# Block-sparse attention and a gated FFN on one core: half of the batches by lists of key blocks instead of dense masked scores

## The chip, the core and the metric

One core of a Trainium2 chip runs the whole program. The metric is device time in microseconds (us); the median of three runs of the kernel before is 308.7 us. Engines in the profile: PE multiplies matrices (PEld loads its weights), DVE and ACT do elementwise work, ACT also exponentials, POOL is the general engine that also issues some transfers, SP only issues transfers. All five work through their own fixed list of instructions in order and wait for each other by semaphores.

## The reference

```python
# q, k, v: (4 batches, 8 heads, 768 positions, 64); blocks of 32 positions, 24 blocks
scores = q @ k.T / 8
mask   = |block_i - block_j| <= 1, or block_i or block_j is 0 or 23,
         or block_j is one of three sampled blocks of block_i (the same for all batches and heads)
attn   = softmax(where(mask, scores, -1e9));  x = attn @ v          # heads side by side: (3072, 512)
xn     = x / rms(x) * rms_g
out    = (silu(xn @ w_gate) * (xn @ w_val)) @ w_out                 # 512 -> 1536 -> 512
```

A row of a block between 1 and 22 attends to at most 8 of the 24 blocks (itself and two neighbours, the first, the last, three sampled); rows of blocks 0 and 23 attend to all.

## The kernel before

The work is cut into *units* of query positions: batch 0 into three units of 128 rows and one of 384, batches 1 to 3 into two of 384 each, ten units in all (0 to 9). Attention runs by pairs of heads.

Attention is dense, and the mask costs no extra instruction: q and k get 24 further columns (kmask and the row of the block matrix, DVE fills `aug`), so that the score product adds -32768 where the mask forbids. For a pair, `load` fetches k, q, v; `fill` casts k and q into `aug`; `turn` transposes `aug` into a slot `X` by a DMA transpose (batch 0 by PE, `tpx`, `evx`); `pad_v` casts v into `vaug`, whose 65th column is 1, so that the weighted sum also gives the softmax's denominator.

- `qk` (L276): scores, 128 keys by up to 384 queries in one matmul; `exp` (L296): ACT takes the exponential of 768 columns of PSUM.
- `av` (L310): 65 columns wide, the exponentials are the weights; `xo` (L321, L322): DVE divides by the denominator.
- `sq` (L335), `rsq` (L343, POOL), `xq` (L350): RMS norm. `tr` (L361) and `cp` transpose the unit by PE for units 0 to 3, `xt` by a DMA transpose for later ones (`NPET = 4`).
- FFN: `proj` (L388) for g and v, `th` (L397, ACT), `uu` (L403) and `hp` (L414, DVE), `yy` (L427) the second product, `yo` (L437) the scaling, then the store.

PSUM has eight banks: scores use two pairs of banks, g bank 4, v bank 5, y bank 6, the weighted sums bank 7. So g and v of one step wait until DVE has read the step before.

No engine order is written by hand. `op(key, engines with costs, dependencies, priority, function, acquires, releases)` describes each step, and a planner in Python picks, step by step, the one that can start first by its own costs and due times; the result is one fixed list for each engine. Batch 0 attention comes first, with little FFN beside it; from unit 3 on, the attention of later units is woven into the FFN of earlier ones; after about 222 us only FFN is left. Loads run on SP in a fixed sequence `seq`, a new one starting when its buffer is free (`raw` has three).

The lines that copy (L108 ACT, L110 POOL, L112 DVE) are those of the helper `copy`.

Of the kernel before, what the change touches and what calls it, by code (L numbers as in the profile page):

```python
# [17 lines left out]
def kernel(  # L18
# [11 lines left out]
):  # L30
    nc = tc.nc
    SIMOUT = None
# [12 lines left out]
    NSLOT, NAUG, NRAW, NOPEN = 5, 2, 3, 2  # L45
# [6 lines left out]
    UNITS += [(b, c, 3) for b in range(1, B) for c in (0, 3)]  # L52
    NU = len(UNITS)
    HG = [(b, c // 3) for b, c, n in UNITS]
# [3 lines left out]
    raw = ctx.enter_context(tc.tile_pool(name="raw", bufs=NRAW))  # L58
    work = ctx.enter_context(tc.tile_pool(name="work", bufs=2))
    psum = ctx.enter_context(tc.tile_pool(name="psum", bufs=1, space=bass.MemoryType.PSUM))  # L60
    PS = psum.tile([P, 8, 512], FP32, name="PS")

# [7 lines left out]
    raws = {}  # L70
    aug = [const.tile([P, 2, 2, NC, P], BF16, name=f"aug{i}") for i in range(NAUG)]
    XA = const.tile([P, NSLOT, 2, 2, S], BF16, name="XA")
    X = [XA[:, i] for i in range(NSLOT)]
    vaug = [const.tile([P, H * NC, D + 2], BF16, name=f"vaug{i}") for i in range(2)]

    def load(g, i):
        b, pr = divmod(g, NP)
        if i == 0:
            raws[g] = raw.tile([P, 3, 2, NC * D], FP32, name="qkv", tag="qkv")
        nc.sync.dma_start(out=raws[g][:, i], in_=(kv, qv, vv)[i][b, :, 2 * pr:2 * pr + 2, :])  # L80
# [9 lines left out]
    A = [raw.tile([P, 3, 2, NC * D], FP32, name="qkv", tag="qkv") for g in range(3)]  # L90
# [23 lines left out]
    zt = const.tile([P, 512], BF16, name="zt")  # L114
# [11 lines left out]
    def idle(n, bk=7):  # L126
# [23 lines left out]
        base=-(NB - 1), pattern=[[0, 32]], channel_multiplier=1)  # L150
    kt_ = bank16(4)[:, 0:S].rearrange("p (c t) -> p c t", t=P)
# [8 lines left out]
    for t in vaug:  # L160
        nc.vector.memset(t[:, :, D:D + 1], 1.0)
# [71 lines left out]

    def fill(g, i, eng):
        copy(eng, aug[g % NAUG][:, i, :, :, 0:D],
             raws[g][:, i].rearrange("p h (c d) -> p h c d", d=D))

    def pad_v(g, eng):
        b, pr = divmod(g, NP)
        src = raws.pop(g) if b else A[g]  # L240
        copy(eng, vaug[b % 2][:, 2 * pr * NC:2 * (pr + 1) * NC, 0:D],
             src[:, 2].rearrange("p h (c d) -> p (h c) d", d=D))
# [21 lines left out]

    pts, xos, xns, hps, mss, xqs, tiles = {}, {}, {}, {}, {}, {}, {}
    KT, FG = {1: 3, 2: 2, 3: 1}, {1: 3, 2: 2, 3: 1}

    def qk(u, pr, g, bk):
        b, c0, nt = UNITS[u]
        x, kt, w = X[(b * NP + pr) % NSLOT], KT[nt], nt * P  # L270
        s_ = PS[:, bk[0]:bk[0] + 2]
        tiles["s", u, pr, g] = s_
        for e in range(2):
            for j in range(kt):
                jt = g * kt + j
                nc.tensor.matmul(  # L276
                    out=s_[:, e, j * w:(j + 1) * w],
                    lhsT=x[0:KQ, 0, e, jt * P:(jt + 1) * P],
                    rhs=x[0:KQ, 1, e, c0 * P:c0 * P + w], start=True, stop=True)

    def exp(u, pr, g):
        b, c0, nt = UNITS[u]
        kt, w = KT[nt], nt * P
        if (u, pr) not in pts:
            if nt == 1:
# [4 lines left out]
                else:  # L290
                    t_ = work.tile([P, 2, NC, 2, w], BF16, name="pt", tag="pt", bufs=NPT)
                pts[u, pr // 2 * 2], pts[u, pr // 2 * 2 + 1] = t_[:, 0], t_[:, 1]
            else:
                pts[u, pr] = work.tile([P, NC, 2, w], BF16, name="pt", tag="pt", bufs=NPT)
# [6 lines left out]
    def av(u, pr, bk):  # L301
        b, c0, nt = UNITS[u]
        pt, va = pts.pop((u, pr)), vaug[b % 2]
# [11 lines left out]
    def xo(u, pr):  # L315
        nt = UNITS[u][2]
        if u not in xos:
            xos[u] = work.tile([P, nt, H, D], FP32, name="xo", tag="xo")
# [4 lines left out]
            out=xos[u][:, :, 2 * pr:2 * pr + 2, :], in0=o_[:, :, :, 0:D],  # L323
            in1=rz.unsqueeze(3).to_broadcast([P, nt, 2, D]), op=ALU.mult)

    def sq(u, t):
        nt = UNITS[u][2]
# [3 lines left out]
        i, z = 0 if nt == 1 else t, slice(0, DM)  # L331
        if nt == 1:
            z = (slice(0, 3 * DM // 4), slice(3 * DM // 4, DM))[t]
        x = xos[u][:, i].rearrange("p h d -> p (h d)")[:, z]
        nc.vector.tensor_tensor_reduce(  # L335
            out=sc[:, z], in0=x, in1=x, scale=1.0 / DM, scalar=mss[u][:, 0:1] if nt == 1 and t else 1e-6,
            op0=ALU.mult, op1=ALU.add, accum_out=mss[u][:, t:t + 1])

    def rsq(u):
        nt = UNITS[u][2]  # L340
        r = work.tile([P, nt], FP32, name="rs", tag="rs")
        x = mss[u][:, 1:2] if nt == 1 else mss[u]
        nc.gpsimd.tensor_tensor(out=r, in0=x, in1=nhalf[:, 0:nt], op=ALU.pow)  # L343
        mss[u] = r

    def xq(u, t):
        nt = UNITS[u][2]
        if u not in xqs:
            xqs[u] = work.tile([P, nt, DM], BF16, name="xq", tag="xq")
        nc.vector.scalar_tensor_tensor(  # L350
            out=xqs[u][:, t, :], in0=xos[u][:, t].rearrange("p h d -> p (h d)"),
# [12 lines left out]
    def cp(u, eng):  # L364
        nt = UNITS[u][2]
        xns[u] = work.tile([P, nt, NP, P], BF16, name="xn", tag="xn", bufs=NXN)
        o, i = xns[u], tiles.pop(("tr", u))[:, 0:nt]
        if eng == "ACT":
            nc.scalar.copy(out=o, in_=i)
        else:  # L370
            nc.vector.tensor_copy(out=o, in_=i)

    def xt(u):
# [4 lines left out]
            in_=xqs[u].rearrange("p t f -> p (t f)"))  # L378

# [27 lines left out]
    def hp(u, f):  # L407
        nt = UNITS[u][2]
        fg = FG[nt]
        if u not in hps:  # L410
            if HG[u] not in hps:
                hps[HG[u]] = work.tile([P, NF, 3 * P], BF16, name="hp", tag="hp", bufs=NHP)
            hps[u] = hps[HG[u]][:, :, UNITS[u][1] % 3 * P:(UNITS[u][1] % 3 + nt) * P]
# [17 lines left out]
    def yo(u, t, h, eng):  # L431
        b, c0, nt = UNITS[u]
        y_ = tiles.pop(("yp", u, t, h))
        n = y_.shape[1]
        o = work.tile([P, n], FP32, name="yo", tag="yo", bufs=3)
# [4 lines left out]
        dst = out[b * S:(b + 1) * S, :].rearrange("(p c) f -> p c f", c=NC)  # L440
        nc.sync.dma_start(out=dst[:, c0 + t, h * n:(h + 1) * n], in_=o)

    NPT, NXN, NHP, NPET = 3, 3, 2, 4
    pools = {n: [0.0] * c for n, c in (
        ("pt", NPT), ("hp", NHP), ("xo", 2), ("xq", 2), ("xn", NXN), ("raw", NRAW), ("va0", 1),
        ("va1", 1), ("th", 2), ("uu", 3))}
    for i in range(NSLOT):
        pools[f"X{i}"] = [0.0]
    for i in range(NAUG):
        pools[f"aug{i}"] = [0.0]  # L450
# [3 lines left out]
    held = {}  # L454
    LAT = {"PE": 0.2, "ACT": 0.16, "DVE": 0.08, "POOL": 0.1, "DMA": 1.9, "DMA2": 2.0}
    ops, end, made = [], {}, {}

    def op(key, engs, deps, prio, fn, acq=(), rel=(), at=0.0):
        o = dict(key=key, engs=engs, deps=deps, prio=prio, fn=fn, acq=acq, rel=rel, at=at,
                 n=len(ops))  # L460
# [5 lines left out]
    def ld0(key, d, fn=None, deps=(), acq=(), rel=()):  # L466
        op(key, {"DMA": d}, list(deps), (0,), fn, acq, rel)
        seq.append(key)

    for g in range(NP - 1):  # L470
        held["raw", g] = "raw"
        pools["raw"].pop()
# [17 lines left out]

    prev = None
    for i in range(NWC + NOC):
# [15 lines left out]
        seq.append(("w", i))  # L508
        if i >= NWC - 1:
            seq += [("ld", NP + i - NWC + 1, j) for j in range(3)]  # L510
    seq += [("ld", g, i) for g in range(2 * NP - 1, B * NP) for i in range(3)]
    in_seq = set(seq)
# [5 lines left out]
    for g in range(NP):  # L518
        a_ = g % NAUG
        rr = [("raw", g)] if g < NP - 1 else []  # L520
# [3 lines left out]
        for n_, (es, lo, hi) in enumerate(QP[g == 0]):  # L524
            dep = ("q2",) if lo == 3 else ("l", 0, 1, n_) if g == 0 else ("l", g, 1)
            pri = (-1, g, 1) if lo == 0 else (2.5, g, lo)
# [4 lines left out]
        for i in range(2):  # L531
            for n_, (es, lo, hi) in enumerate((KP, QP)[i][g == 0]):
# [3 lines left out]
                else:  # L536
                    pri = (-1, g, 1) if lo == 0 else (2.5, g, lo)
# [16 lines left out]
    for r_ in "KQR":  # L554
        for a_ in range(2):
            pools[f"a{r_}{a_}"] = [0.0]
    held["aK0", 0] = "aK0"
# [3 lines left out]
    for g in range(NP, B * NP):  # L561
        b, pr = divmod(g, NP)
        gate = {NP: 2, NP + 1: 3, NP + 2: 4, NP + 3: 5}.get(g)
        for i in range(3):
            def ld(e, p, g=g, i=i, gate=gate):
# [3 lines left out]
            op(("ld", g, i), {"DMA": 1.1}, [("w", gate)] if gate is not None and i == 0 else [],  # L569
               (1,), ld, [("raw", g)] if i == 0 else [])  # L570
# [4 lines left out]
            else:  # L575
                op(("pv", g), {"DVE": 0.57}, [("ld", g, 2), ("fill", g, 0), ("fill", g, 1)],
                   (4, g, 2), lambda e, p, g=g: pad_v(g, e), [(f"va{b % 2}", b)], [("raw", g)])
        op(("turn", g), {"DMA": 4.6}, [("fill", g, 0), ("fill", g, 1)], (-1, g),
           lambda e, p, g=g: turn(g), [(f"X{g % NSLOT}", g)], [(f"aug{g % NAUG}", (g, False))])

# [9 lines left out]

    for u, (b, c0, nt) in enumerate(UNITS):
        w, last = nt * P, c0 + nt == NC
        ng = NC // KT[nt]
        for pr in range(NP):
            g0 = b * NP + pr
            pk = pr // 2 if nt == 1 else pr
            ptn = ("hp", "ph") if u == 0 and pk == 1 else ("pt", (u, pk))
            for g in range(ng):
                op(("qk", u, pr, g), {"PE": 2 * KT[nt] * mm(w)}, dep0(g0, b, c0, nt, KT[nt], g),
                   (2 if u else 0.5, u, pr, g), lambda e, p, a=(u, pr, g): qk(*a, p),  # L600
                   [(S3 if u < NOPEN else S_, ("s", u, pr, g)), ptn],
                   [(f"X{g0 % NSLOT}", g0)] if last and g == ng - 1 else [])
                op(("exp", u, pr, g), {"ACT": 0.075 + 2 * KT[nt] * w / 1200.0},
                   [("qk", u, pr, g)], (3, u, pr, g), lambda e, p, a=(u, pr, g): exp(*a),
                   [], [(None, ("s", u, pr, g))])
            op(("av", u, pr), {"PE": nt * 12 * 0.0325},
               [("exp", u, pr, g) for g in range(ng)] + [("pv", g0)]
               + ([("av", u, pr - 1)] if nt == 1 and pr % 2 else []), (1, u, pr),
               lambda e, p, a=(u, pr): av(*a, p), [([(7,)] + [(6,)] * (u < 3), ("o", u, pr)), ("xo", u)],
               ([ptn] if nt > 1 or pr % 2 else []) + ([(f"va{b % 2}", b)] if last and pr == NP - 1 else []))  # L610
            op(("xo", u, pr), {"DVE": 0.4 + w / 960.0}, [("av", u, pr)], (0, u, pr),
               lambda e, p, a=(u, pr): xo(*a), [], [(None, ("o", u, pr))])
        ns = max(nt, 2)
        for t in range(ns):
# [185 lines left out]
```

## Time and profile before

| | us |
|---|---|
| runs | 308.39, 308.70, 309.43 (median 308.7) |
| span of the profiled execution (first to last instruction) | 307.2 |
| median less span: what lies around it | 1.5 |
| PE, ACT, DVE, POOL busy | 299.6, 203.7, 192.3, 24.4 |
| ACT in the dense exponentials (192 of 128x768, about 812 ns each) | 145.8 |

The profiled execution has a span of its own and no separate time; changes are worked out in it and carried to the median. Busy PE time counts modelled ends of pipelined matmuls; the chain of work that ended last, in order of time, gives the spacing of matmuls. A line of a group reads: line, engine, operation, out<-in, shapes, count, then busy us, mean ns of one, idle time before them and what ended it. A line of a stretch reads: from:to, length, then busy time (and instructions) of PE, PEld, DVE, ACT, POOL, granted clock, share of the DMA engines, GB/s.

### The profile page before, as it was taken

What the parts mean: (1) busy time and instruction counts of PE and PEld (TensorE: products, weight loads), DVE (VectorE), ACT (ScalarE), POOL (GpSimd) and SP (SyncE); (2) the same over time, 40 slices, a digit from 0 to 9 for tenths busy, and PEclk for the clock granted to TensorE, in tenths of its full rate; (3) what the DMA queues carried; (4) which work ended last, traced back from release to release, by engine and by line L of the source; (5) the groups of instructions that cost most, each with busy time, mean ns of one, the idle gap of its engine ahead of it and who ended that gap; (6) DMA issues with size and microseconds to landing.
All of it is one profiled execution on the core that took longest, in us unless ns stands there. A gap on an engine that the chain in (4) does not pass through costs nothing.

```text
span 307.2 us, 7350 instructions
## 1 busy us (share of the span) xinstructions
PE 299.6 (98%) x3033; PEld 200.2 (65%) x3062; DVE 192.3 (63%) x435; ACT 203.7 (66%) x319; POOL 24.4 (8%) x43
## 2 busy tenths in 40 slices
PE   8999999999999999999999999999999999999994
PEld 7998888766666566666666666666666546556543
DVE  6687766857779678756754753674389607727500
ACT  5999875678977878787877787878833143233221
POOL 3566000100001001001000100010000000000000
PEclk9999999999999999999999999999999999999999
DMA  7999999999999999940894030003010050010022
GB/s 207 370 231 172 215 268 228 228 333 247 262 285 271 227 205 222 242 155 3 173 157 101 0 87 2 34 3 85 2 36 1 20 158 12 0 70 0 0 105 104
DMA packets 70661, 42.42 MB, mean 138 GB/s; under 512 B 48356, under 2 KB 67556, under 8 KB 70628
## 3 DMA queue, kind: packets, MB, share of 16 engines
q1 hardware_dynamic: 64528, 37.17, 49.2%
q0 software_dynamic: 5792, 4.72, 10.0%
q8 instruction: 24, 0.39, 0.6%
q10 hardware_dynamic: 308, 0.07, 0.1%
q14 instruction: 9, 0.07, 0.1%
HBM read 28.57 MB, written 6.29 MB: 114 GB/s over the span
## 4 chain that ended last, share of the span: by engine, by line
PE 96%; ACT 2%; issue 1%; DVE 0%; ACTq 0%
PE PS L388 40%; PE PS L276 20%; PE PS L427 20%; PE PS L310 12%; PE PS L258 2%; ACT pt L296 1%; PE PS L128 1%; PE PS L361 0%; ACT th L397 0%; PE PS L153 0%; ACT yo L437 0%; PE PS L183 0%; DVE zt L115 0%; ACTq L437 0%
## 5 line engine op out<-in xcount | busy, mean ns | idle before, releaser
L296 ACT ACTIVATE pt<-PS 128x768 bf16<-128x768 f32 x188 | 142.8, 812 | 32.2 <-PE PS L276 31.5
L403 DVE SCALAR_TENSOR_TENSOR uu<-th,PS 128x384 bf16<-128x384 bf16 x96 | 53.0, 554 | 58.7 <-ACT th L397 55.7
L276 PE MATMUL PS<-XA 88*128 88x384 bf16 (+1 forms) x480 | 81.1, 293 | 0.7 <-ACT pt L296 0.6
L388 PE MATMUL PS<-xn,wv 128*128 128x384 bf16 (+1 forms) x480 | 75.5, 293 | 0.0
L388 PE MATMUL PS<-xn,wg 128*128 128x384 bf16 (+1 forms) x480 | 75.1, 294 | 0.0
L397 ACT ACTIVATE th<-PS 128x384 bf16<-128x384 f32 x96 | 47.2, 493 | 34.8 <-PE PS L388 32.1
L427 PE MATMUL PS<-wo,hp 128*128 128x512 bf16 (+1 forms) x271 | 65.4, 370 | 1.5
L414 DVE TENSOR_TENSOR hp<-uu,PS 128x384 bf16<-128x384 bf16 x96 | 51.4, 551 | 14.2 <-PE PS L388 14.0
L388 PEld LDWEIGHTS <-wv 128*128 128x128 bf16 x480 | 41.6, 97 | 23.3
L388 PEld LDWEIGHTS <-wg 128*128 128x128 bf16 x480 | 41.4, 98 | 22.5
L276 PEld LDWEIGHTS <-XA 88*128 88x128 bf16 x480 | 39.2, 97 | 21.4 <-issue 1.8
L427 PEld LDWEIGHTS <-hp 128*128 128x128 bf16 x300 | 29.1, 98 | 27.0
L310 PEld LDWEIGHTS <-pt 128*128 128x128 bf16 x1128 | 40.5, 97 | 5.8
L310 PE MATMUL PS<-vaug,pt 128*128 128x65 bf16 x1128 | 42.1, 193 | 0.0
L437 ACT ACTIVATE yo<-PS 128x512 f32<-128x512 f32 (+1 forms) x22 | 12.7, 578 | 27.9 <-PE PS L427 27.2
L343 POOL TENSOR_TENSOR rs<-ms,nhalf 128x3 f32<-128x3 f32 (+1 forms) x10 | 7.9, 785 | 203.8 <-DVE ms L335 203.8
L322 DVE TENSOR_TENSOR xo<-PS,rz 128x384 f32<-128x384 f32 (+1 forms) x40 | 19.1, 478 | 1.4
L350 DVE SCALAR_TENSOR_TENSOR xq<-xo,rs,gB 128x512 bf16<-128x512 f32 x24 | 17.3, 747 | 2.3 <-POOL rs L343 2.3
L335 DVE CUSTOM_DVE_ANT_0 sc<-xo 128x512 bf16<-128x512 f32 (+1 forms) x24 | 16.1, 669 | 0.2
L321 DVE RECIPROCAL rz<-PS 128x6 f32<-128x6 f32 (+1 forms) x40 | 7.4, 186 | 12.8 <-PE PS L310 12.6
L112 DVE CAST aug<-qkv 128x768 bf16<-128x768 f32 (+1 forms) x28 | 14.5, 538 | 0.1
L112 DVE COPY XA<-PS 88x768 bf16<-88x768 bf16 (+2 forms) x17 | 8.4, 516 | 2.3 <-PE PS L258 2.2
(60 smaller groups left out, 74.5 us busy)
## 6 DMA issues: line engine op xcount, KB each, us to landing
out_dram<-yo SPq DMA_DIRECT2D x23, 256.0 KB, 2.4
qkv<-in_v_dram SPq DMA_DIRECT2D x15, 384.0 KB, 6.1
qkv<-in_k_dram SPq DMA_DIRECT2D x14, 384.0 KB, 5.6
qkv<-in_q_dram SPq DMA_DIRECT2D x12, 384.0 KB, 5.7
wg<-in_moe_w_gate_dram POOLq DMA_DIRECT2D x4, 384.0 KB, 7.3
wv<-in_moe_w_val_dram POOLq DMA_DIRECT2D x4, 384.0 KB, 8.4
wo<-in_moe_w_out_dram POOLq DMA_DIRECT2D x2, 768.0 KB, 19.0
q<-in_q_dram SPq DMA_DIRECT2D x1, 768.0 KB
```

Of the source, the lines that this page charges most:

```text
L112: nc.vector.tensor_copy(out=out, in_=in_)
L276: nc.tensor.matmul(out=s_[:, e, j * w:(j + 1) * w], lhsT=x[0:KQ, 0, e, jt * P:(jt + 1) * P], rhs=x[0:KQ, 1, e, c0 * P:c0 * P + w], start=T ...
L296: nc.scalar.activation(out=pts[u, pr][:, g * kt:(g + 1) * kt].rearrange("p j e w -> p e j w"), in_=s_[:, :, 0:kt * w].rearrange("p e (j w) ...
L310: nc.tensor.matmul(out=o_[:, t, e, :], lhsT=pt[:, jt, e, t * P:(t + 1) * P], rhs=va[:, (2 * pr + e) * NC + jt, 0:D + 1], start=(jt == 0), ...
L322: nc.vector.tensor_tensor(out=xos[u][:, :, 2 * pr:2 * pr + 2, :], in0=o_[:, :, :, 0:D], in1=rz.unsqueeze(3).to_broadcast([P, nt, 2, D]), o ...
L335: nc.vector.tensor_tensor_reduce(out=sc[:, z], in0=x, in1=x, scale=1.0 / DM, scalar=mss[u][:, 0:1] if nt == 1 and t else 1e-6, op0=ALU.mul ...
L350: nc.vector.scalar_tensor_tensor(out=xqs[u][:, t, :], in0=xos[u][:, t].rearrange("p h d -> p (h d)"), scalar=mss[u][:, t:t + 1], in1=gB, o ...
L388: nc.tensor.matmul(out=p_[:, j, :].rearrange("p (t w) -> p t w", w=P), lhsT=w_[:, c, f_ * P:(f_ + 1) * P], rhs=xns[u][:, :, c, :], start=( ...
L397: nc.scalar.activation(out=t_, in_=tiles["gp", u, f], func=AF.Tanh, scale=0.5)
L403: nc.vector.scalar_tensor_tensor(out=t_, in0=tiles.pop(("th", u, f)), scalar=1.0, in1=tiles.pop(("gp", u, f)), op0=ALU.add, op1=ALU.mult)
L414: nc.vector.tensor_tensor(out=hps[u][:, f * fg:(f + 1) * fg, :], in0=tiles.pop(("uu", u, f)), in1=tiles.pop(("vp", u, f)), op=ALU.mult)
L427: nc.tensor.matmul(out=tiles["yp", u, t, h], lhsT=hps[u][:, f, t * P:(t + 1) * P], rhs=wo[:, f, x], start=(f == 0), stop=(f == NF - 1))
```

## The change

Batches 0 and 1 stay dense (`dk`, `dexp`, `dav`, `dxo` are the old `qk`, `exp`, `av`, `xo`). Batches 2 and 3 are cut otherwise: a tile is 128 query rows of four blocks, five tiles of blocks 1 to 20 and one (`AT`, number 5) of blocks 0, 23, 21, 22. Units 6 and 8 hold tiles 5, 0, 1, units 7 and 9 tiles 2, 3, 4.

For a listed tile, six groups of 128 keys are put together (`kg`): for each of its four query blocks x its three sampled blocks and one fixed neighbour (groups 0 to 3), and two groups that two query blocks share (neighbours and the blocks 0 and 23). Where a sampled block is already covered by a neighbour, a global block or an earlier sample, its V index points to 32 rows of zeros, so that it counts in neither the sum nor the denominator.

- A table is computed on the chip from the sampled blocks (`table`, some 45 small DVE instructions and four POOL iotas); 66 offsets are loaded into registers of POOL (44) and ACT (22) (`table_regs`).
- K, Q: loaded in natural layout, cast (`fill_k`, `fill_q`), one DMA transpose each for a batch. `kg_fixed` copies the neighbours (any of DVE, ACT, POOL), `kg_sampled` copies one sampled block of 16x2 columns for all pairs of heads from an address in a register: samples 0 and 1 on POOL, 2 on ACT. `q_diag` puts the queries of two heads block-diagonally (`QBD`, its zeros are written once).
- V: cast with the column of ones, stored to DRAM as rows of 8x65 values (`store_v`). For each group x, POOL issues a gather of 128 such rows by the index column (`gather_v`); the shared groups are plain loads from the same rows on SP (`pair_v`).
- Scores: 64 columns for groups 0 to 3, 128 for the shared two, `exp` 512 elements at a time. For tile 5 the 2 global blocks meet all six 128-key groups of the transposed K (`qka`) and the tile's own lists.
- The exponentials go to cleared places (`zero`): the weights are block-sparse, and the zeros stay.
- Units 4 and 5 are transposed by PE (`NPET = 6`); `xn` has two buffers instead of three; from unit 6 on `sq` may be on ACT; output stores are planned as steps of SP.
- All of this lies in the dense batches' buffers: the transposed K and Q in slots 3 and 4 of `X`, the key groups in slots 0 and 2, `QBD` in slot 1, the gathered V in the table's buffer, the rest of the raw buffer and batch 1's V buffer, the exponentials over the dense ones. Each has to wait until its dense user is done.

The core of the diff (`...` where lines are left out):

```diff
-    NSLOT, NAUG, NRAW, NOPEN = 5, 2, 3, 2
+    NR, NHP, NXN, NYO, NPET = NRND, 2, 2, 3, 6
+    NSLOT, NAUG, NOPEN, NDB = 5, 2, 2, 2
+    NPT, NPA, NQB, NKG, NVG, NRAW = 3, 1, 3, 2, 3, 3
...
-    UNITS += [(b, c, 3) for b in range(1, B) for c in (0, 3)]
+    UNITS += [(b, c, 3) for b in range(1, NDB) for c in (0, 3)]
+    ND = len(UNITS)
+    for b in range(NDB, B):
+        UNITS += [(b, (5, 0, 1), 3), (b, (2, 3, 4), 3)]
...
+    def zero(i, eng):
+        for z in zeros(i):
+            (nc.vector if eng == "DVE" else nc.gpsimd).memset(z, 0.0)
+    def turn_k(b):
+        KTs[b] = KTB
+        nc.sync.dma_start_transpose(
+            out=KTs[b].rearrange("p a (n x) -> p (a n) x", x=P), in_=KROW.rearrange("p a c t x -> p (a c t x)"))
+    def kg_sampled(b, n, xs, eng):
+        kg = new_kg(b, n).rearrange("p x a s j c -> p x a c s j")
+        kt = KTs[b].rearrange("p a (c y) -> p a c y", c=2)
+        for x, r in xs:
+            kb = koff[(blocks(n)[x] - 1) * NR + r]
+            copy(eng, kg[:, x, :, :, r, :], kt[:, :, :, bass.ds(kb, 16)])
+    def gather_v(b, n, x):
+        c_ = blocks(n)[x] - 1
+        nc.gpsimd.indirect_dma_start(
+            out=new_vg(b, n)[:, x, :], out_offset=None, in_=vrows[b][:, :],
+            in_offset=bass.IndirectOffsetOnAxis(ap=idx[:, c_:c_ + 1], axis=0))
+    def q_diag(b, n, eng):
...
+                copy(eng, t_[hs, i:i + m, h].rearrange("p i a x -> p a i x"), src)
+    def qk(b, n, pp, bk):
...
+            for i in range(4):
+                qmm(o_[:, :, i * 32:(i + 1) * 32], kg[:, i, pr], qb, i, 1, pr)
+            for g in range(2):
+                lo = P + g * 64
+                qmm(o_[:, :, lo:lo + 64], kg[:, 4 + g, pr], qb, 2 * g, 2, pr)
+    def av(b, n, pp, bk):
...
+            for x, v_ in enumerate(vs):
+                nc.tensor.matmul(
+                    out=o_[:, a, :], lhsT=p_[:, a, x * P:(x + 1) * P], rhs=v_,
+                    start=(x == 0), stop=(x == len(vs) - 1))
...
+                op(("gv",) + T + (x,), {"POOL": 1.05}, [("st", b), ("ix", 7)], (1.1, order, x),
+                   lambda e, p, a=T + (x,): gather_v(*a), [("vg", T)])
+                    e_ = "ACT" if r == 2 else "POOL"
+                    op(("kd",) + T + (r, xs[0]), {e_: (0.8, 0.7)[e_ == "ACT"]},
+                       kdep + [("rg", e_, p) for p in range(len(REGS[e_]))], (1.1, order, -2, r),
+                       lambda e, p, a=T, z=[(x, r) for x in xs]: kg_sampled(*a, z, e), [("kg", T)], [("X3", ("KT", b))])
+        op(("zr", i), {"DVE": 1.3, "POOL": 1.9} if i <= NPT else {"DVE": 0.7, "POOL": 1.1},
+           done0 if i <= NPT else [("dk", ND - 1, 2, ng3 - 1)], (1, i), lambda e, p, i=i: zero(i, e))
```

## The prediction

> **What bounds the kernel now.** I read the page first (busy shares, slices, chain), then the chain in order of time for the real price of one matmul, then busy time by stretch, and last the groups and single instructions for the prices of work that moves.
>
> ```profile
> span 307.2 us, 7350 instructions
> ...
> PE 299.6 (98%) x3033; PEld 200.2 (65%) x3062; DVE 192.3 (63%) x435; ACT 203.7 (66%) x319; POOL 24.4 (8%) x43
> ...
> PE 96%; ACT 2%; issue 1%; DVE 0%; ACTq 0%
> PE PS L388 40%; PE PS L276 20%; PE PS L427 20%; PE PS L310 12%; PE PS L258 2%; ACT pt L296 1%; PE PS L128 1%; PE PS L361 0%; ACT th L397 0%; PE PS L153 0%; ACT yo L437 0%; PE PS L183 0%; DVE zt L115 0%; ACTq L437 0%
> ```
>
> The chain that ended last is 96% PE matmuls: whatever leaves PE shortens the run, as long as the other engines keep feeding it. A group's mean (293 ns) is latency in a pipeline, so the price has to come from the chain in order of time (start, duration, line, count):
>
> ```profile
> 58.04 1.34 PE PS L388 x24
> ...
> 181.29 1.15 PE PS L310 x36
> 182.44 0.65 PE PS L276 x4
> 183.09 1.30 PE PS L388 x8
> ```
>
> So 162.5 ns for 384 columns, 55.8 ns for 128 (the x24 at 58.04) and 31.9 ns for 65. Does PE starve when others are busy? In the stretches (length, then PE, PEld, DVE, ACT, POOL busy):
>
> ```profile
> 60.00:70.00 10.00, 9.89 (x100) 6.24 (x100) 6.48 (x13) 7.94 (x11) 0.00 (x0) 1.00 1.02 339
> 90.00:100.00 10.00, 9.81 (x147) 7.07 (x146) 9.33 (x23) 6.74 (x12) 1.04 (x1) 1.00 1.10 272
> 110.00:120.00 10.00, 9.95 (x117) 6.63 (x117) 8.79 (x21) 7.37 (x12) 0.85 (x1) 1.00 1.13 201
> ```
>
> With DVE at 88 to 93% PE lost 0 to 0.14 us in 10; the clock stood at 1.00.
>
> **PE's part of the change.** Counts are from the order in which each kernel's instructions stand. Batches 2 and 3 lose 4 units x 4 pairs x 12 = 192 dense score matmuls of 384 columns: 192 x 162.5 ns = 31.2 us. They get 176 of 64 columns (31.9 ns, the 65-column row) = 5.6 us and 136 of 128 columns (55.8 ns) = 7.6 us. Weighted sums go from 576 to 624 matmuls, as a listed tile still reads 6 blocks of 128 keys and the tile of the global rows 9: 48 x 31.9 ns = 1.5 us. Units 4 and 5 now transpose on PE instead of by DMA: 24 more at about 51 ns (L361's 0.4% of the chain over 24) = 1.2 us. The 960 L388 and 300 L427 matmuls stay. Net: 31.2 - 5.6 - 7.6 - 1.5 - 1.2 = **15.3 us less PE**. With nothing else, the profiled span of 307.2 becomes 291.9; the median of the runs, 308.7, lies 1.5 us above that span, so 293.4.
>
> **What has to hide beside it.** Nearest prices: ACT 597 ns (512 elements), 384 (256), about 280 (128); POOL copies fit 190 ns + 0.83 ns an element (507 for 384, 827 for 768); DVE rows as they are.
>
> ```profile
> L403 DVE SCALAR_TENSOR_TENSOR uu<-th,PS 128x384 bf16<-128x384 bf16 x96 | 53.0, 554 | 58.7 <-ACT th L397 55.7
> L397 ACT ACTIVATE th<-PS 128x384 bf16<-128x384 f32 x96 | 47.2, 493 | 34.8 <-PE PS L388 32.1
> L350 DVE SCALAR_TENSOR_TENSOR xq<-xo,rs,gB 128x512 bf16<-128x512 f32 x24 | 17.3, 747 | 2.3 <-POOL rs L343 2.3
> L211 POOL DMA_DIRECT2D wg<-in_moe_w_gate_dram x4 | 3.3, 818 | 0.0
> L110 POOL CAST aug<-wo 128x768 bf16<-128x768 f32 x1 | 0.8, 827 | 0.6 <-PE PS L258 0.6
> ```
>
> *The listed stage*, between the 28th and the 67th hp product (units 4 to 7 in the FFN), summed over the order:
> - PE 103.8 us.
> - DVE 90.0: 39 uu x 0.554 = 21.6, 39 hp 21.5, 20 xo with reciprocals 12.1, 12 xq 9.0, 5 sq 3.8, 3 yo 2.1, 32 key and query copies inside SBUF at most 14.7 (0.33 to 0.59 each, priced as a plain one-element stream; at the pace of the f32 casts, 553 ns for 768, half), the rest 5.2.
> - ACT 83.2: 39 th 19.2, exps 33.8 (36 of 512, 32 smaller), 54 key copies 17.0, 6 fills 5.5, squares and yo 7.1, one dense exp. 96 dense exps of 812 ns (78 us) are gone; that is what pays for the copies.
> - POOL, from the first query copy to its end: 41 gathers, 76 key copies x 0.295 = 22.4, 17 larger copies 8.7, 9 small ops x 0.878 = 7.9. A gather's price is in no row: nearest is the plain issue (0.74 to 0.95); I take 1.0, so 80 us against 102 us of PE before the last weighted sum. Below it could be 0.75 (70 us); above nothing bounds it, see the rivals. Tile by tile POOL then finishes keys 0 to 17 us ahead of PE, tightest in the first three listed tiles.
>
> PE stays longest, but DVE's spare time falls from about 38% to 13%, and both g and v wait on it through two PSUM banks. By the stretches above a DVE this full costs 0 to 1.4% of 104 us, 0 to 1.5 us. POOL is new beside it, and one row shows what that does:
>
> ```profile
> L110 POOL CAST aug<-q x4: 502/504/855, 19.4 to 23.3; 128x384 bf16<-128x384 f32 x4
> ...
> 23.26 0.55 DVE L335 CUSTOM_DVE_ANT_0 sc<-xo 128x384 bf16<-128x384 f32 x1
> ...
> 23.32 0.85 POOL L110 CAST aug<-q 128x384 bf16<-128x384 f32 x1 [0.18 <-PE PS L258]
> ```
>
> Three of four equal POOL casts took 0.50 us; the one that started 0.06 us after a DVE square took 0.85: 0.35 us lost once. The stage has about 55 such DVE instructions (xq, sq, copies inside SBUF) and 100 POOL copies. If each of the 55 met a POOL copy and lost 0.35 us, DVE would have 90 + 19 = 109 us and pass PE by 5; if the toll falls on POOL, its lead pays. I take 3.0 us of stalls, range 0 to 7.
>
> [...]
>
> *Changeover.* Between the last dense score matmul and the first listed one PE has 44 L388, 18 L427 and 36 L310: 7.2 + 3.9 + 1.2 = 12.3 us. POOL has 8 key copies 2.4, a gather 1.0, eight clears of 6656 elements (no row: POOL's 0.83 ns an element and 0.1 each) 6.3, six query copies 2.8: 12.5 us, in that order, and the last feeds PE. Clears at 0.5 or 1.25 ns an element give 10 or 15 us: a stall of 0 to 3; I take 1.5. Without that cover all 12.5 us would show.
>
> *Dense stage.* About 45 tiny DVE instructions build the table (rows of 60 to 160 ns: 5 us in a stage where DVE had a quarter free), POOL and ACT load 66 offsets into registers (no row; between 0 and 0.2 us each, 22 of them on ACT between dense exps, which wait behind). 0 to 3 us; I take 0.5.
>
> *Queues.* SP carries the loads as before, two V stores, pair loads, and 12 transposes instead of 18 (4.4 us median of the key/query ones, 6.2 at most). K and V of batch 2 can load once batch 1's last V is copied, about 74 us of PE work in, against 119 needed: covered. For batch 3 the key transpose waits for batch 2's last key copy (POOL 30 us into the stage), lands by 37, POOL has its key copies done at 38, and its first scores stand at 49: covered by 11 us. Cover gone, a late transpose would cost its 4.4 us. DMA was under 40% busy in every stretch of 10 us after 170 us, so the 44 gathers of 133 KB have room. Ends are as before: the same all-FFN tail.
>
> Sum: 308.7 - 15.3 + 0.5 + 1.5 + 3.0 = **298.4 us**.
>
> **Rivals.**
> 1. DVE takes over as the bound (chance 0.20): the 5 us above plus the changeover's 3 and the dense stage's 3 stand, 293.4 + 11 = 304. For it: 90 of 104 us is only the average; from the 52nd to the 55th hp it is 6.7 against PE's 6.6. Against: DVE at 93% cost PE 0.14 us in 10.
> 2. POOL takes over, the one that ends slower (0.15): the gather's price decides. PE's list is fixed, so each tile waits for its four gathers. POOL's total is 39 us + 4 for register sums + 41 gathers against 99 us (102 less about 3 for landing): from 1.4 us a gather PE waits, and from 1.8 us the gain is gone (43 + 74 = 117, 18 late). At 2.0 us: 125 - 99 = 26, so 293.4 + 26 = 319 us. [...] Against: plain issues of 128 x 4 pieces took 0.74 to 0.95.
> 3. It does not do what it says (0.05): a short listed matmul costs a weight load's 97 ns instead, 312 x 97 = 30.3 us, and with the 2.7 us of other additions PE gains nothing: 310 + stalls. Against: L310 has one weight load for each 65 columns and runs at 31.9 ns.
>
> **How the numbers follow.** My case has 0.60, with 293.4 to 303.5 by its own bounds (0 to 10). A measurement of this kernel tells 0.3%, 0.9 us. Faster: 0.60 + nearly all of rival 1 + gathers priced under 1.7 us = 0.80. Within: 0.03. Slower: the rest of rivals 2 and 3, 0.17. Range: 292.5 (listed matmuls 1 us cheaper) to 308.5 (rival 1 and part of 2), leaving out about 2 in 10.
>
> **What would show it.** Right: PE busy near 284 us, chain still over 90% PE, the score rows at 32 and 56 ns in the chain, PE idle beyond 2 us only at 110 to 125 us. Wrong: waits of PE on DVE hp or uu above 6 us in total (rival 1); waits of PE on gathers or POOL key copies and a POOL without idle time (rival 2); gathers above 1.4 us; or the chain passing through SP transposes between batches 2 and 3.

## The result, and the profile after

The changed kernel took 307.93 us (median of 20 executions, 303.99 to 312.24) beside 309.06 us before (20 executions, 308.39 to 310.41). The ratio is 0.9928, 95% interval 0.9906 to 0.995; it leaves out executions more than 1.5% above the fastest of their kernel, seven of the changed kernel's 20, so it lies below the quotient of the medians. By the ratio that is 2.2 us faster, by the medians 1.1, where 10.3 were forecast; the time is inside the range, near its slow end. The profiled execution took 306.13 us, with a span of 304.4; it is 1.8 us faster than the median. Executions of the changed kernel spread over 8 us, those of before over 2.

PE's 40 slices before:

```profile
PE   8999999999999999999999999999999999999994
```

From the page of the changed kernel: span, busy time, the slices of PE and of its granted clock, the chain.

```profile
span 304.4 us, 8288 instructions
...
PE 289.0 (95%) x3231; PEld 198.4 (65%) x3254; DVE 207.8 (68%) x483; ACT 189.3 (62%) x377; POOL 125.0 (41%) x224
...
PE   8999999998999999489999999999999999999995
...
PEclk9999999999999999689999999999999999999999
...
PE 24%; POOL 5%; issue 3%; DVE 0%; POOLq 0%; ACT 0%; ACTq 0%
```

PE's slices are as full as before but for the 10th (68 to 76 us, a little) and the 17th and 18th (122 to 137 us), where the clock drops too. The chain's shares add up to about a third: it loses its track, so it can't be read as before. By stretch (length, then PE, PEld, DVE, ACT, POOL busy, granted clock, DMA share, GB/s):

```profile
110.00:120.00 10.00, 9.75 (x89) 5.88 (x88) 5.32 (x11) 8.57 (x19) 9.39 (x15) 1.00 0.76 170
120.00:130.00 10.00, 5.80 (x53) 3.30 (x51) 8.97 (x10) 3.02 (x5) 8.63 (x15) 0.74 0.93 183
130.00:140.00 10.00, 9.23 (x70) 5.52 (x71) 6.02 (x15) 5.47 (x15) 1.86 (x3) 0.92 0.85 182
```

From 120 to 130 us DVE is busy for 8.97 us with only ten instructions. Instruction by instruction (start, duration, engine, line, operation):

```profile
119.01 5.94 POOL L463 MEMSET PTC<- 128x1536 bf16 x8
...
119.67 5.69 DVE L146 CAST AUG<-RAWC 128x768 bf16<-128x768 f32 x1
...
125.29 0.53 DVE L766 SCALAR_TENSOR_TENSOR uu<-th,PS 128x384 bf16<-128x384 bf16 x1
...
125.87 2.72 PE L751 MATMUL PS<-xn,wg 128*128 128x384 bf16 x8 [4.08 <-DVE uu L766]
```

One cast on DVE, 0.55 us elsewhere, took 5.69: it began 0.66 us after the first of eight clears on POOL and ended 0.41 us after the last (124.95). (The shape in the line of clears is that of the first; the eight differ and come to 6656 elements.) uu stood behind it on DVE, g's matmul waited for uu, and PE idled 4.08 us. The view of PE's waits (us in total, times, longest) has it first:

```profile
PE PS L751 <- DVE uu L766: 4.3, 2, 4.1
```

The clock record shows half speed from 124.8 to 131.6 us.

Groups, by shape (busy time, mean ns of one, idle before):

```profile
L716 DVE SCALAR_TENSOR_TENSOR xq<-XO,rs,gB 128x512 bf16<-128x512 f32 x24 | 19.9, 856 | 2.5 <-POOL rs L709 2.5
...
L144 POOL COPY XC<-XC 128x128 bf16 x88 | 25.3, 357 | 0.1
L570 POOL DMA_INDIRECT VAC<-vrows,idx x16 | 16.6, 1040 | 4.2 <-issue 2.4 <-PE PS L751 0.6 <-PE PS L790 0.3
```

To place the loss I follow PE's own order: the start of each weight load, less the sum of the prices on record for all matmuls ahead of it (32 ns for 64 and 65 columns, 55.8 for 128, 162.5 for 384, 216.5 for 512). This is the time that PE has lost by then. By those prices PE's whole list is 296.6 us before and 281.5 after, 15.1 less. In the listed stage the matmuls of 64 and of 65 columns in fact start 29 ns apart, not 32; over some 750 of them that is about 2 us that the table counts as work, so its listed column is about 2 us too low in every kernel with lists. The loss grows as follows in three stretches of that list (e3 and e7 have 70 matmuls more in theirs and are left out): dense stage, 15 to 110 us of PE work (21 to 119 us of the span after); changeover, 110 to 120 (119 to 137); listed stage, 120 to 220 (137 to 239):

| profiled run | dense | changeover | listed |
|---|---|---|---|
| before | 1.4 | 0.0 | 0.0 |
| after | 2.9 | 7.9 | 2.2 |
| e1: cast on ACT | 5.6 | 0.9 | 3.2 |
| e2: clears on DVE | 3.7 | 2.8 | 3.0 |
| e4: gaps between clears | 5.4 | 1.1 | 3.2 |
| e5: e1, register loads split | 3.6 | 0.9 | 3.3 |
| e6: register loads split alone | 4.1 | 7.8 | 4.1 |
| e8: e5, loads clear of a transpose | 3.2 | 0.9 | 5.0 |
| e9: e8, input copy shared | 2.5 | 0.9 | 3.9 |

### The profile page after: what moved, and what is told of

It is laid out like the page before. It is cut to its first block, busy times and chain, and to the rows that moved or that the text cites. A ratio compares the mean times of both kernels' runs of the same rounds, so it can differ in the third digit from the quotient of the medians.

```text
span 304.4 us, 8288 instructions
## 1 busy us (share of the span) xinstructions
PE 289.0 (95%) x3231; PEld 198.4 (65%) x3254; DVE 207.8 (68%) x483; ACT 189.3 (62%) x377; POOL 125.0 (41%) x224
## 5 line engine op out<-in xcount | busy, mean ns | idle before, releaser
L341 ACT ACTIVATE PTC<-PS 128x768 bf16<-128x768 f32 x92 | 70.6, 816 | 12.2 <-PE PS L320 11.9
L320 PE MATMUL PS<-XC 88*128 88x128 bf16 (+1 forms) x288 | 43.2, 276 | 1.8 <-ACT xn L142 1.2
L144 POOL COPY XC<-XC 128x128 bf16 (+3 forms) x108 | 37.1, 407 | 7.9 <-issue 3.4
L320 PEld LDWEIGHTS <-XC 88*128 88x128 bf16 x288 | 22.2, 99 | 10.1 <-issue 2.5
L630 ACT ACTIVATE PTC<-PS 128x512 bf16<-128x512 f32 x40 | 22.3, 601 | 6.8 <-PE PS L603 6.8
L672 PEld LDWEIGHTS <-PTC 128*128 128x128 bf16 x624 | 21.6, 97 | 3.1 <-issue 0.4
L716 DVE SCALAR_TENSOR_TENSOR xq<-XO,rs,gB 128x512 bf16<-128x512 f32 x24 | 19.9, 856 | 2.5 <-POOL rs L709 2.5
L355 PEld LDWEIGHTS <-PTC 128*128 128x128 bf16 x552 | 20.0, 97 | 1.8
L355 PE MATMUL PS<-VAC,PTC 128*128 128x65 bf16 x552 | 21.1, 193 | 0.0
L142 ACT COPY XC<-XC 128x128 bf16 (+2 forms) x61 | 18.5, 396 | 3.5 <-PE PS L601 3.1
L570 POOL DMA_INDIRECT VAC<-vrows,idx x16 | 16.6, 1040 | 4.2 <-issue 2.4
```

What stands on the lines that cost most here:

```text
L144: nc.gpsimd.tensor_copy(out=out, in_=in_)
L320: nc.tensor.matmul(out=s_[:, e, j * w:(j + 1) * w], lhsT=x[0:KQ, 0, e, jt * P:(jt + 1) * P], rhs=x[0:KQ, 1, e, c0 * P:c0 * P + w], start=T ...
L341: nc.scalar.activation(out=pts[u, pr][:, g * kt:(g + 1) * kt].rearrange("p j e w -> p e j w"), in_=s_[:, :, 0:kt * w].rearrange("p e (j w) ...
L355: nc.tensor.matmul(out=o_[:, t, e, :], lhsT=pt[:, jt, e, t * P:(t + 1) * P], rhs=va[:, (2 * pr + e) * NC + jt, 0:D + 1], start=(jt == 0), ...
L570: nc.gpsimd.indirect_dma_start(out=new_vg(b, n)[:, x, :], out_offset=None, in_=vrows[b][:, :], in_offset=bass.IndirectOffsetOnAxis(ap=idx[ ...
L630: nc.scalar.activation(out=o_, in_=i_, func=AF.Exp, scale=SCALE)
```

## The experiments

Theory 1: DVE's cast from SBUF to SBUF and POOL's clears exclude each other, and DVE does not come in between POOL's instructions as long as they follow without a gap. Theory 2: the transfers of that stretch slow the cast. Theory 3: the half clock behind the stall is a loss by itself. Line numbers shift by a few from kernel to kernel.

**e1, the cast on ACT**

```diff
     def fill_k(b, hf, c, eng):
+        if (b, hf, c) == (3, 0, 0):
+            eng = "ACT"
```

> The cast of the third key block of the last batch, which took 5.69 us on DVE beside a run of eight POOL clears, goes to ACT; nothing else changes. [...] Theory 2 (the cast was slow through the transfers of that stretch): the cast is long on ACT too, and the time stays at about 307.

302.41 us (301.94 to 303.72), ratio to before 0.98, interval 0.9775 to 0.9824. The instructions beside the clears:

```profile
120.69 5.94 POOL L463 MEMSET PTC<- 128x1536 bf16 x8
...
122.08 0.84 ACT L142 CAST AUG<-RAWC 128x768 bf16<-128x768 f32 x1
122.23 0.56 DVE L768 SCALAR_TENSOR_TENSOR uu<-th,PS 128x384 bf16<-128x384 bf16 x1 [0.78 <-ACT th L762]
...
123.11 0.56 DVE L368 TENSOR_TENSOR XO<-PS,rz 128x384 f32<-128x384 f32 x1
...
124.24 0.97 DVE L463 MEMSET PTC<- 128x768 uint32 x2
```

The casts on ACT take 0.84 us beside the same run of clears; uu and xo (both read PSUM; 0.56 us each) and DVE's own two clears (no input; 0.97 us, as in the changed kernel, where they stand behind POOL's) keep their length. Changeover loss 0.9 us instead of 7.9. Theory 1, by which the stall goes when the cast leaves DVE, holds, Theory 2 falls; e2 and e4 test both on DVE's cast itself. A new wait shows, in the dense stage: PE's waits of this kernel, and the instructions there,

```profile
PE PS L753 <- DVE uu L768: 2.7, 2, 2.5
```

```profile
58.85 0.49 ACT L762 ACTIVATE th<-PS 128x384 bf16<-128x384 f32 x1 [5.22 <-issue]
...
59.37 0.55 DVE L768 SCALAR_TENSOR_TENSOR uu<-th,PS 128x384 bf16<-128x384 bf16 x1 [3.16 <-ACT th L762]
...
59.98 0.83 PE L753 MATMUL PS<-xn,wg 128*128 128x128 bf16 x12 [2.45 <-DVE uu L768]
```

ACT stands still for 5.22 us with "issue" as the cause. The trace's own records show the second register load of eleven offsets there, from 53.12 to 58.72 us. In the changed kernel the same load took 3.25 us.

**e2, all clears on DVE**

```diff
     def zero(i, eng):
+        if i <= NPT:
+            eng = "DVE"
```

> All clears of the exponent buffers go to DVE; POOL does none of them. Theory 1: no run of POOL clears, so the cast falls from 5.69 to about 0.55 us; DVE has some 3 us of clears more, part of them ahead of the first uu: 300 to 303 us. Theory 2 (transfers slow the cast): the cast stays near 5.7 us and the time at 307 or more.

303.93 us (301.63 to 305.23), ratio 0.9833 (0.9806 to 0.986).

```profile
119.58 0.55 DVE L146 CAST AUG<-RAWC 128x768 bf16<-128x768 f32 x1
```

The cast has its usual length, with the same transfers under way. DVE's clears now stand in its own queue (2.06 us of them ahead of the next uu) and cost a part of the gain back: changeover 2.8.

**e3, matmuls in the stall**

```diff
         if o["fn"] is not None:
             o["fn"](e, bk)
+        if o["key"] == ("v", 4, 4):
+            idle(70, 0)
```

> 70 matmuls of 128 columns whose result nobody reads stand ahead of the matmul that waits for the first uu of the listed stage, so that PE is not idle in the stall. The stall itself stays. Theory 3 (the half clock behind the stall is a loss of its own, 6.8 us at half speed = about 3.4 us): no slice of the record under 0.9, time about 303.5 to 304.5 us. If the clock costs nothing beside the stall, since DVE or POOL set the pace there: about 307 to 308.

307.15 us (305.23 to 310.31), ratio 0.9923 (0.9894 to 0.9953): no difference from the changed kernel, although the clock stayed at 1.00. It is inconclusive by itself, because in its profiled run the register load took 5.63 us and the dense stage lost 5.3. e7 repeats it without that.

**e4, gaps between POOL's clears**

```diff
     def zero(i, eng):
+        if i in (2, 3):
+            gate = KROW[:, 0, 0, 0, 0:1] if i == 2 else PTB[1][:, 0, 32:33]
+            nc.gpsimd.tensor_copy(out=scr[:, 12:13], in_=gate)
```

> Two copies of one element on POOL between its clears, the first of which waits for DVE's cast and the second for DVE's own clear: the same clears on the same engine, with a gap in which DVE can start. Theory 1: the cast ends within 0.6 us of the end of the POOL clear it met, instead of at the end of all eight, and the stall falls from 4.1 to 1.5 us or less: about 301 to 303 us. Theory 2 (transfers): the cast is as long as before, POOL waits for it, and the time is 307 or more.

302.32 us (301.21 to 306.5), ratio 0.9791 (0.9751 to 0.983).

```profile
120.56 1.86 POOL L466 MEMSET PTC<- 128x1536 bf16 x2
...
121.23 1.62 DVE L146 CAST AUG<-RAWC 128x768 bf16<-128x768 f32 x1
...
122.91 0.19 POOL L464 COPY scr<-AUG 128x1 bf16<-128x1 bf16 x1 [0.48 <-DVE AUG L146]
123.04 1.83 POOL L466 MEMSET PTC<- 128x1536 bf16 x2
```

Same clears, same engines; POOL now stops after two. They end at 122.42 and the cast at 122.85, 0.43 us later, as it ended 0.41 us after the run of eight. The time is that of e1. It is the unbroken run that DVE waits for.

**e5, e1 with ACT's register loads split**

```diff
+    def table_regs(eng, part, some=None):
+        if eng == "ACT" and some is None:
+            return
         ...
+        if o["key"][:2] == ("th", 3) and o["key"][2] < 11:
+            table_regs("ACT", 0, (2 * NS + 2 * o["key"][2], 2 * NS + 2 * o["key"][2] + 2))
```

> The cast on ACT as in the first experiment, and ACT's two register loads of eleven values each replaced by eleven loads of two values, one behind each of the first eleven tanh steps of unit 3. Theory A (the register loads hold ACT, 2.6 us and 3.3 to 5.6 us at a stretch, and PE waited 2.5 us for the tanh behind the second): a load of two values takes about 0.5 us, PE's wait of 2.5 us near 57 to 60 us goes, nothing comes in its place, and the time falls by 2 to 2.7 us from 302.4 to about 300. Theory B (the load is long because ACT or its fetch is held up by the transposes in flight then, whatever it loads): a small load is long too when it meets them, and the time stays at 302 to 303.

300.21 us (299.54 to 301.4), ratio 0.9713 (0.9688 to 0.9737): 2.2 us below e1, the intervals apart. Loads of two took 0.49 to 0.69 us, but two near 90 us took 0.86 and 1.48: both theories hold in part. PE's waits, the longest two; the one of 2.5 us on uu is gone:

```profile
PE PS L605 <- ACT PTC L661: 1.6, 3, 0.7
PE PS L320 <- ACT xn L142: 1.2, 1, 1.2
```

**e6, the register loads split alone; e7, e6 with the 70 matmuls of e3**

e6 has the edits of e5 without that of e1; e7 adds to e6:

```diff
+        if o["key"] == ("v", 4, 4):
+            idle(70, 0)
```

> The changed kernel with its DVE cast as it was, and only ACT's register loads split into eleven loads of two values. The stall beside POOL's clears stays (about 4 us, and the half clock behind it). Theory A: 305.3 to 306.5 against 307.9, and a narrower spread than 304 to 312, since the length of the load varies from run to run. Theory B, or a load that costs the path nothing: 307 to 308.

> The kernel of the run before in this call, with the 70 matmuls that nobody reads in the stall, so that its difference to that run is the half clock alone. If the half clock costs its 3.4 us on the path: 302 to 303. From the traces of the changed kernel and of the third experiment, counted behind the dense stage, 2.2 us: about 303.5. If another engine sets the pace there, as the third experiment's total seemed to say: no difference.

e6: 307.32 us (305.53 to 307.68), ratio 0.9927 (0.9901 to 0.9953). The gain of 1.4 to 2.6 us did not come; the spread is narrower, over six executions. In its profiled run two small loads took 1.91 and 1.29 us, and PE lost 1.3 us there; and the changed kernel's own profiled run had only the 3.25 us load to gain from.

e7: 305.31 us (303.74 to 305.91), ratio 0.9857 (0.9831 to 0.9882), 2.0 us below e6, the intervals apart. Dense stage alike in both profiles (4.1 and 4.0 us lost). The clock's slices of e6:

```profile
PEclk9999999999999999699999999999999999999999
```

and of e7:

```profile
PEclk9999999999999999999999999999999999999999
```

So in this pair the half clock is a loss by itself, some 2 us of the 2.9 that the 5.7 us of work at half speed make, and the same stall costs less when PE is kept at work in it. The size rests on this pair alone: e3 showed no gain, and among the changed kernel's 20 executions the nine with a granted clock up to 0.989 and the eleven from 0.992 up have nearly the same median (308.0 and 307.9 us).

**e8, the loads clear of the transpose near 89 us; e9, e8 with the input copy shared**

e8 against e5, then e9 against e8:

```diff
-        if o["key"][:2] == ("th", 3) and o["key"][2] < 11:
-            ...
+        if o["key"][:2] == ("th", 3) and o["key"][2] < 8:
+            cut = (0, 2, 5, 8, 11, 14, 17, 20, 22)[o["key"][2]:]
+            table_regs("ACT", 0, (2 * NS + cut[0], 2 * NS + cut[1]))
```

```diff
     def cp(u, eng):
         ...
+        if u == 3:
+            t_ = tiles.pop(("tr", u))
+            copy("ACT", xns[u][:, 0:2], t_[:, 0:2])
+            copy("DVE", xns[u][:, 2:3], t_[:, 2:3])
         ...
```

> As the fifth experiment, with ACT's register loads behind the first eight tanh steps of unit 3 (two or three values each), so that none lies in the stretch of the transpose that begins near 89 us, in which loads of two values took 0.86 to 1.91 us instead of 0.50. If a load is long because a transpose that moves data at the same time holds it up: every load takes 0.5 to 0.8 us, PE loses some 0.8 us less between 85 and 95 us, about 299.5 against 300.2. If the length goes by something else, some loads stay over 1 us and the time stays at 300.2. A load of three beside an early transpose near 75 us may be hit instead.

> As the kernel before it in this call, and the copy of unit 3's transposed input out of PSUM (1536 columns on ACT, 1.44 us, for which PE waited 1.2 us near 71 us) shared: two thirds on ACT, one third on DVE. ACT's part should take some 1.0 us, so PE's wait falls to about 0.7 and the time by 0.4 to 0.5 us; if another use of the same bank ends last, no difference.

e8: 300.12 us (299.16 to 301.86), ratio 0.9711 (0.9684 to 0.9739). Every load took 0.49 to 0.81 us, also one of three values beside the transpose near 73 us (0.81); the time is that of e5. In its profiled run the dense stage lost 0.4 us less, and the listed stage 1.6 more: one wait for a POOL copy took 1.9 us (0.7 in e5), and behind it the clock stood at half from 181.59 to 185.01 us, some 1.7 us of work lost. From its page of PE's waits and its clock's slices:

```profile
PE PS L605 <- POOL XC L144: 1.9, 1, 1.9
...
PEclk9999999999999999999999997999999999999999
```

e9: 299.64 us (297.31 to 300.08), ratio 0.968 (0.9652 to 0.9708). PE's wait for the copy fell from 1.2 to 0.6 us; the interval overlaps that of e8. It is the fastest kernel of this study, 9.9 us under before by the ratio, and close to the forecast.

## Why the prediction was wrong, point by point

**PE's part: right.** PE's list is 15.1 us shorter by the prices on record (15.3 forecast). By start to start, a score matmul of 64 columns takes 29 ns and one of 128 takes 56. With 29 ns for the listed 64 and 65 columns the list is about 2 us shorter still. PE busy is 289.0 us, not 284: in this view time lost in short waits and at half clock counts as busy, so it was a poor witness. The third rival (a weight load's 97 ns for each short matmul) falls.

**The changeover: the step that failed.** It stood at 1.5 us, with 3 as its end, worked out as POOL's length (12.5) against PE's cover (12.3). POOL's clears were priced well, 5.94 us against 6.3. What was missing is what their run does to DVE: the step put that at nothing. The loss was 7.9 us, 6.4 above its term: 4.1 of PE idle, most of the rest the half clock after it. e1, e2 and e4 remove it in three ways and leave 0.9 to 2.8 us; in e1 and e4, with nothing moved onto DVE, the step's own 1.5 would have been near enough.

**The toll of one encounter: the price behind that.** I took 0.35 us from one POOL cast beside a single DVE square, and spread it over 55 encounters in the listed stage. Here one encounter cost 5.14 us (5.69 - 0.55), because the other side was eight instructions long. The clear under way when the cast began ended 0.74 us later; the cast waited for all that was left of the run, 5.28 us. So the toll has to be taken from the run, not from one instruction. Not every DVE instruction paid it: in e1 uu (0.56 us) and xo (0.56 us), each with one input in PSUM and one in SBUF, and DVE's two clears (0.97 us) kept their length beside the same run.

**Rival 1** (DVE becomes the bound) named the mechanism, but put it in the listed stage, as a sum of many small tolls. There PE lost 2.2 us in the changed kernel and 3.0 to 5.0 in the others, against 3.0 forecast (0 to 7); with the matmuls at 29 ns, about 2 more in each, which their lower price gives back. One bound of the 3.0 was misread: the stretch from 90 to 100 us before has PE 0.19 us short of 10, not 0.14, so a DVE that full could cost 2.0 us rather than 1.5. PE's waits on uu came to 4.3 us in all, below the 6 that I had set as its sign, and 4.1 of them were one wait. DVE's copies inside SBUF, at 0.33 to 0.59 us an estimate of mine, took 0.32 to 0.53 in the means of their groups.

**The dense stage: too low.** 0.5 us forecast (0 to 3); 1.5 more than before in the changed kernel, 1.8 to 4.1 more in the other kernels up to e8. Up to 0.2 us for a register load was a guess of mine that no row shows; ACT's 22 took 5.85 us, 0.27 each, as two instructions of 2.60 and 3.25 us, and in e1 the second took 5.60. In the changed kernel's profile PE lost only 0.3 us around the second load, in e1's 2.6. The small loads of e5 took 0.25 us a value where nothing held them up (0.49 for two). A further 1.2 us is PE's wait for the copy of unit 3's transposed input, which e9 halves; it was in no term. POOL's three loads (10.1 us) fell where POOL had nothing else to do.

**Rival 2** (the gather's price) falls: gathers took 0.96 to 1.04 us on POOL in the mean of their three groups, against 1.0 taken; one of the 44 took 1.52. Key copies took 357 ns each, 295 taken. PE waited for a POOL copy once in the changed kernel, for 0.5 us.

**The sum.** Before to after by the table and the terms: -15.1 PE, +1.5 dense, +7.9 changeover, +2.2 listed, +1.0 ahead of the dense stretch (the first loads, which differ from run to run), together -2.5; the spans differ by 2.8. With the changeover at its forecast 1.5 the rest of the prediction would have given some 6 us more. With the stall gone (e1) 302.4 us are left against 298.4 forecast; by the table nearly all of that is the dense stage, 4.1 us more than before instead of 0.5.

**Still open:** what decides whether a register load is held up in a given run, whether that makes the spread of the changed kernel, and why its median lies 1.8 us above its profiled execution.

## What to carry to other kernels

Before long runs of POOL work are placed beside DVE copies from SBUF to SBUF, price the meeting by the whole unbroken run of POOL instructions (5.28 us of it were left here, and the cast waited for them all), and look at who stands behind the DVE instruction in its queue; put that copy on ACT (0.84 us in e1), or break the run with an instruction that waits for DVE (1.62 us in e4). A stall on PE can be paid again in its clock afterwards: here one of 4.1 us was, with 6.8 us at half speed. Loads of values into registers are real work on the engine that makes them, here 0.25 us each: place them where nobody waits for that engine. Splitting them brought 2.2 us in e5 over e1, and nothing in e6.

## What the runs showed of the hardware that was not expected

- DVE did not get in between eight POOL clears, although each was an instruction of its own (5.69 us instead of 0.55). The same with copies: at 143.26 us of the changed kernel an xq of 0.75 us took 2.14 and ended only beside the last of a run of POOL copies.
- Register loads on ACT took longer beside some of the transposes by DMA. Those of e1, e3 and e4 met the transpose issued from 54 to 58 us, took 5.60, 5.63 and 5.46 us, and ended 0.30, 0.51 and 0.31 us after that transpose's issue ended. The same load in the changed kernel and in e2 began at 53.79 and 53.91 us, also beside transposes, and took only 3.25 and 3.04. Small loads near 90 us took up to 1.91 us beside another transpose and 0.49 without. Some beside the shorter transpose near 75 us were not held up. What decides it is not shown.
- In the changed kernel PE's clock fell to half 3.0 us after its last work and stayed there for 6.8 us, 5.7 of them after work had begun again. The length of the wait alone does not decide: in e8 it fell behind a wait of 1.9 us (178.59 to 180.48), when work had begun again, and in e1, e3 and e4 waits of 2.3 to 2.5 us left it at 1.00.
